# Every SBUF operand at a multiple of 128 bytes, and fourteen layouts for the operands of a squared-ReLU MLP

## The chip, the cores and the metric

The kernel runs on one core of one Trainium2 chip. The core has TensorE (PE in the profile), VectorE (DVE), ScalarE (ACT), GpSimd (POOL) and SyncE (SP, which issues most DMAs). On-chip memory is SBUF, 128 partitions wide; TensorE accumulates in PSUM. The metric is the device time of one execution in microseconds (us). Before the change it is 448.87 us, the median of three runs (448.64 to 449.05).

A matmul here has two operands in SBUF. The *stationary* one, 128 x 128 numbers, is loaded into the array by a weight load (LDWEIGHTS, the row PEld of the profile); the *moving* one, 128 partitions x N columns, is streamed through it by the MATMUL. Every matmul of this kernel is preceded by a weight load of its own.

## The reference: what is computed

Two blocks read the same x (2048 tokens, width 448), and a gate mixes them:

```python
g = sigmoid((x * gate_w).sum(-1, keepdims=True))
a = linear_attention(x, wqkv, wo)         # 16 heads, phi(t) = max(t,0) + min(exp(t),1) + 1e-6
h = relu(x @ w1 + b1) ** 2                # 448 -> 1792
b = h @ w2 + b2                           # 1792 -> 448
out = g * a + (1 - g) * b
```

All is float32. Each operand is split into a high part, rounded to the type float32r, and a low part that holds the rest; a product is then three matmuls (high x high, high x low, low x high).

## The kernel before

**Tiling.** Tokens go in four blocks b of 512. The 1792 hidden features are fourteen feature tiles f of 128, and each block meets them in two halves of seven (NH = 7): first b = 0, 1, 2, 3 with f = 0 to 6, then b = 3, 0, 1, 2 with f = 7 to 13.

**The two MLP products.** `up(b, f)` (line 206) makes `h_ps`: the stationary operand is a 128-column piece of `w1`, the moving one `xh` or `xl`, 512 columns; eleven matmuls. `hidden` takes ReLU (line 210) and square (211) on ACT and splits the result into `hh` and `hl` on DVE (a cast by line 59, a subtraction by line 62). `down(b, f)` (line 235) adds into `o_ps`: for each of four token tiles the stationary operand is 128 columns of `hh` or `hl`, the moving one a half of `w2_f`, 448 columns; twelve matmuls. So each feature tile has 4 x 11 = 44 matmuls up and 4 x 12 = 48 down, and the fourteen together 616 and 672.

**The other products** run by line 74: keys `k_ps` (176 matmuls of 450 columns), the Gram products `g_ps` (176 of 448), queries `q_ps` (160 of 512), the attention output `a_ps` (176 of 448), and some small ones: `m_ps` and `d_ps`, and by lines 356 and 335 `kv_ps` (32 of 112) and `z_ps`.

**Order.** The instruction order on every engine is fixed when the program is built. TensorE works on `up(b, f)`, then on `down(b, f - 1)`, then on a piece of the attention block; in the second half it is `denominators`, `scaled` and `attention`. DVE, ACT and SP follow in the same order, each engine strictly one instruction after the other. An instruction that waits for a semaphore holds up everything behind it on its engine.

**Memory.** Long-lived tiles lie in the pool `keep`, one after the other. Loaded raw data and short-lived results share the pool `work`: NSLOT = 16 slots of 2048 bytes a partition. Whoever takes a slot waits until the last reader of its previous content is done. `tmp` and later `late` hold the operands of the attention block.

**Where the operands start.** Byte addresses in a partition, modulo 128, as the built program has them:

| operand | stationary or moving | before | after |
|---|---|---|---|
| `xh`, `xl` | moving in up and q, stationary in k | 0 | 0 |
| `w1`, tiles fl = 0 to 3 of a half | stationary | 0 | 0, 16, 32, 48 |
| `w1`, tiles fl = 4 to 6 | stationary | 64 | 64, 80, 96 |
| `hh`, `hl` | stationary | 96 | 0 |
| `w2_f` | moving | 0 | by f, see the change |
| `wq_s` | stationary | 96 | 0 |
| `m_s` (a) | moving | 0, 8, 16, 24, 32, 40, 48 by piece | 0 |
| `qh`, `ql` (a) | stationary | 96 | 0 |
| `wk_s` (k) | moving | 0, 8, ... 48 by piece | the same |
| `nh`, `nl` (g) / `ph`, `pl` | stationary / moving | 96 / 96 | 0 / 0 |

Of the kernel before, what the change touches and what calls it, by code (L numbers as in the profile page):

```python
# [7 lines left out]
F = mybir.dt.float32  # L8
R = mybir.dt.float32r
# [4 lines left out]
S, D, FF, H = 2048, 448, 1792, 16  # L14
DH = D // H
P = 128
# [14 lines left out]
def gated_mix_kernel(ctx: ExitStack, tc: tile.TileContext, xt, xn, wk, wq, wv, wo, w1a, w1b, w2, b1, b2, hmask,  # L31
# [2 lines left out]
    act, dve, pool, pe, sp = nc.scalar, nc.vector, nc.gpsimd, nc.tensor, nc.sync  # L34

    keep = ctx.enter_context(tc.tile_pool(name="keep", bufs=1))
    work = ctx.enter_context(tc.tile_pool(name="work", bufs=1, side="right"))
    acc_p = ctx.enter_context(tc.tile_pool(name="acc_p", bufs=4, space=PSUM))
    mm_p = ctx.enter_context(tc.tile_pool(name="mm_p", bufs=2, space=PSUM))
    ms_p = ctx.enter_context(tc.tile_pool(name="ms_p", bufs=2, space=PSUM))  # L40

    NSLOT, NLATE = 16, 15

    def slot(shape, dt, name):
        return work.tile(shape, dt, name=name, tag="s", bufs=NSLOT)
# [77 lines left out]

    def split_w1(h, g, c, hi_eng=act):
        if c == 0:
            w1_s[h, g] = keep.tile([P, 7, (TB, 3 * P)[g]], R, name=f"w1_{h}{g}", tag=f"w1{g}", bufs=1)
        split_w(w1_s[h, g], c, w1_raw.pop((h, g, c)), hi_eng, dve)

    w2_s, w2_raw = {}, {}

    def load_w2(f):
# [1 line left out]
        load(w2_raw[f], w2[f])  # L133

    def split_w2(f):
        w2_s[f] = keep.tile([P, 2, D], R, name=f"w2_{f}", tag="w2", bufs=NH)
        split_hi(act, w2_s[f][:, 0], w2_raw[f])
        split_lo(dve, w2_s[f][:, 1], w2_raw.pop(f), w2_s[f][:, 0])

    xn_raw = {}  # L140

# [16 lines left out]
    for _ in range(18):  # L158
        pe.matmul(warm_ps[:, :256], warm[:, :P], warm, start=True, stop=True)

    side = keep.tile([P, 2], F, name="side")
    dve.memset(side[:64, 0:1], -1.0)
    dve.memset(side[:64, 1:2], 0.0)
    dve.memset(side[64:], 1.0)
# [1 line left out]
    for c in range(4):  # L166
# [3 lines left out]
            load_x(0, c, TB // 2, TB)  # L170
        else:
            load_x(0, c)
    b1_s = keep.tile([P, NF], F, name="b1_s")
    load(b1_s, b1)
    load_w2(0)
    load_w2(1)
# [2 lines left out]

    b2_s = keep.tile([P, D], F, name="b2_s")  # L180
    hm = keep.tile([P, P], R, name="hm")
    half = keep.tile([P, 2], F, name="half")
    ones = keep.tile([P, 2], F, name="ones")
    dve.memset(ones, 1.0)
    ksum = keep.tile([P, D], F, name="ksum")
    logit = keep.tile([P, NT], F, name="logit")
    gate = keep.tile([P, 2, NT], F, name="gate")
    part = [keep.tile([P, D], F, name=f"part{t}") for t in range(NT)]

# [6 lines left out]
    def up_chunk(ps, b, f, c):  # L196
        h, fl = divmod(f, NH)
        g, i = divmod(fl, 4)
        w, cols = w1_s[h, g], slice(i * P, (i + 1) * P)
        xh, xl = xs[b]  # L200
        if c < 3:
            terms = [(w[:, c, cols], xh[:, c]), (w[:, c, cols], xl[:, c]), (w[:, 4 + c, cols], xh[:, c])]
        else:
            terms = [(w[:, 3, cols], xh[:, 3]), (w[:, 3, cols], xl[:, 3])]
        for n, (a, m) in enumerate(terms):
            pe.matmul(ps, a, m, start=(c == 0 and n == 0), stop=(c == 3 and n == 1))  # L206

    def hidden(ps, b, f):
        r = slot([P, TB], F, f"hr{b}_{f}")
        act.activation(r, ps, AF.Relu, bias=b1_s[:, f:f + 1])  # L210
        act.activation(r, r, AF.Square)  # L211
        h = slot([P, TB], R, f"hh{b}_{f}")
        lo = slot([P, TB], R, f"hl{b}_{f}")
        split_hi(dve, h, r)
        split_lo(dve, lo, r, h)
        hs[f] = (h, lo)

    def up(b, f):
        ps = mm_p.tile([P, 512], F, name=f"h_ps{b}_{f}", tag="mm")
# [4 lines left out]
    o_ps = {}  # L224

    def down(b, f, tiles=range(4)):
        h, lo = hs[f]
        w = w2_s[f]
        for i in tiles:
            if f % NH == 0:  # L230
                o_ps[i] = acc_p.tile([P, 512], F, name=f"o_ps{b}_{f}_{i}", tag="acc")
            cols = slice(i * P, (i + 1) * P)
            terms = [(h[:, cols], w[:, 0]), (h[:, cols], w[:, 1]), (lo[:, cols], w[:, 0])]
            for n, (a, m) in enumerate(terms):
                pe.matmul(o_ps[i][:, :D], a, m, start=(f % NH == 0 and n == 0),  # L235
                          stop=(f % NH == NH - 1 and n == 2))
# [83 lines left out]
        split_lo(dve, second[0], second[1], second[0])  # L320


    zc = keep.tile([P, 4], F, name="zc")

# [173 lines left out]
    for f in range(2, 4):  # L500
        hidden(first[f], 0, f)

    wk_s = keep.tile([P, 7, D + 2], R, name="wk_s", tag="wkm", bufs=1)

    load_xn(0)
    load_w2(2)
# [108 lines left out]
    for n, b in enumerate(order):  # L615
        then = order[n + 1] if n + 1 < NB else None
        for f in range(NF - NH, NF):
            fl = f - NH
            run_todo()
            up(b, f)  # L620
            if fl:
                if n + 1 < NB or f + 1 < NF:
                    down(b, f - 1)
            elif n == 0:
                down(b, NH - 1)
                half_done(b)
            else:
                down(order[n - 1], NF - 1)
                for i in range(4):
                    finish(order[n - 1], i)  # L630
            if n == 0:
                if fl < 4:
                    todo += queries(b, (3, 0, 1, 2)[fl])
                if fl == 0:
                    for c in range(4):
                        load_w1(1, 1, c)
                    kv_product()
                    phase1.close()
                    late = ctx.enter_context(tc.tile_pool(name="late", bufs=1, side="right", reuse_waits="tile"))
                    m_s = keep.tile([P, 7, 450], R, name="m_s", tag="wkm", bufs=1)  # L640
                    for j in range(2):
                        load_wo(j)
                if fl == 1:
                    for c in range(4):
                        split_w1(1, 1, c)
                if fl in (1, 2):
                    for j in range(2 * fl - 2, 2 * fl):
                        split_wo(j)
                        todo += m_product(j)
                    if fl == 1:  # L650
                        for j in range(2, 4):
                            load_wo(j)
                if fl < 2:
                    load_w2(NH + 5 + fl)
                    split_w2(NH + 4 + fl)
                if fl == 2:
                    split_w2(NH + 6)
                if fl == 4:
                    todo += denominators(b)
                if fl == 5:  # L660
                    for c in range(4):
                        scaled(b, c)
                if fl == 6:
                    for i in range(4):
                        attention(b, i)
            else:
                if fl == 0:
                    todo += denominators(b)
                if fl == 1:
                    for c in range(4):  # L670
                        scaled(b, c)
                if 2 <= fl < 6:
                    attention(b, fl - 2)
            if then is not None:
                if fl < 2:
                    load_x(then, 2 * fl)
                    load_x(then, 2 * fl + 1)
                if 1 <= fl < 3:
                    split_x(then, 2 * fl - 2)
                    split_x(then, 2 * fl - 1)  # L680
                if n and 3 <= fl:
                    todo += queries(then, (3, 0, 1, 2)[fl - 3])
                if n == 0 and fl in (5, 6):
                    for c in ((3, 0), (1, 2))[fl - 5]:
                        todo += queries(then, c)
# [56 lines left out]
```

## Time and profile before

| | |
|---|---|
| median of three runs | 448.87 us |
| the profiled execution | 448.76 us |
| its span (first to last instruction) | 447.0 us |
| PE busy | 439.9 us, 2054 matmuls |
| PEld busy | 381.2 us |
| DVE / ACT / POOL busy | 267.8 / 172.4 / 58.5 us |
| granted TensorE clock | 0.999 |

The profiled execution lies 0.11 us under the median, inside the spread of the runs. Outside the span lie 1.8 us. In the profile a row names source line, engine, operation and tiles (`o_ps<-w,hh` reads `w2` and `hh` and writes `o_ps`; the numbers of blocks and tiles are left out), then shapes and a count. The recorded duration of a matmul (368 or 394 ns) is a latency, from its start to the end of its drain: matmuls overlap, and what one costs is the distance from its start to the next one's start. The chain of waits gives such distances directly: a piece of the chain with its start, its length and the count of instructions in it.

### The profile page before, as it was taken

To read this page: it belongs to the slowest core of one execution; us is meant where nothing else is said; L and a number is where in the kernel's file an instruction comes from. 1 tells how busy PE (TensorE), PEld (TensorE's weight loads), DVE (VectorE), ACT (ScalarE), POOL (GpSimd) and SP (SyncE) were. 2 spreads that over 40 slices of the span, in tenths; PEclk is the share of its full clock that TensorE was granted. 3 is DMA by queue.
4 is the path that set the end of the run, shared out by engine and by line. 5 is a ranking of instruction groups with operands and counts; after the bars stand their busy time and mean duration, and the time that the engine had idled before them with its cause. 6 is when DMAs were issued, how large, how long until landed. Compare 5 with 4: busy or idle time off the path is not lost.

```text
span 447.0 us, 5489 instructions
## 1 busy us (share of the span) xinstructions
PE 439.9 (98%) x2054; PEld 381.2 (85%) x2054; DVE 267.8 (60%) x452; ACT 172.4 (39%) x298; POOL 58.5 (13%) x75
## 2 busy tenths in 40 slices
PE   8999999999999999999999989999999999999996
PEld 6888898888888888888888868888888898888885
DVE  5968445442687326772466678788355974549423
ACT  5945235331455123542344334335232443234221
POOL 0243124110342005320002420000000000000000
PEclk9999999999999999999999999999999999999999
DMA  7651210022031211252145311040100501002002
GB/s 270 186 179 52 84 44 25 23 65 70 0 116 31 66 44 40 70 137 55 42 123 146 72 37 24 1 165 12 26 0 0 177 1 25 0 0 84 0 1 82
DMA packets 18315, 28.77 MB, mean 64 GB/s; under 512 B 2880, under 2 KB 12784, under 8 KB 18288
## 3 DMA queue, kind: packets, MB, share of 16 engines
q1 hardware_dynamic: 17072, 26.81, 19.7%
q0 software_dynamic: 1216, 1.61, 1.9%
q8 instruction: 16, 0.26, 0.3%
q14 instruction: 11, 0.09, 0.1%
HBM read 22.09 MB, written 3.67 MB: 58 GB/s over the span
## 4 chain that ended last, share of the span: by engine, by line
PE 93%; DVE 3%; ACT 2%; issue 1%; DMA 1%; SPq 0%; DVEq 0%; ACTq 0%
PE h_ps L206 30%; PE o_ps L235 30%; PE q_ps L74 8%; PE a_ps L74 8%; PE g_ps L74 8%; PE k_ps L74 7%; PE kv_ps L356 1%; DMA xr<-in_xt 1%; ACT hr L210 1%; PE m_ps L74 1%; DVE hh L59 0%; ACT hr L211 0%; DVE r L254 0%; ACT ph L55 0%; DVE r L255 0%
## 5 line engine op out<-in xcount | busy, mean ns | idle before, releaser
L235 PE MATMUL o_ps<-w,hh 128*128 128x448 f32 x448 | 127.9, 368 | 0.5 <-DVE hh L59 0.5
L206 PE MATMUL h_ps<-xh,w 128*128 128x512 f32 x392 | 127.9, 394 | 0.2
L235 PEld LDWEIGHTS o_ps<-w,hh 128*128 128x128 f32 x448 | 84.0, 188 | 11.8 <-DVE hh L59 1.2
L206 PE MATMUL h_ps<-xl,w 128*128 128x512 f32 x224 | 88.2, 394 | 0.0
L206 PEld LDWEIGHTS h_ps<-xh,w 128*128 128x128 f32 x392 | 73.7, 188 | 16.5 <-ACT xh L55 0.6
L235 PE MATMUL o_ps<-w,hl 128*128 128x448 f32 x224 | 80.8, 369 | 0.0
L210 ACT ACTIVATE hr<-h_ps,b_s 128x512 f32<-128x512 f32 x56 | 38.2, 683 | 101.7 <-PE h_ps L206 99.9
L59 DVE CAST hh<-hr 128x512 fp32r<-128x512 f32 x56 | 25.3, 451 | 43.1 <-ACT hr L211 42.4
L206 PEld LDWEIGHTS h_ps<-xl,w 128*128 128x128 f32 x224 | 42.1, 188 | 8.7
L235 PEld LDWEIGHTS o_ps<-w,hl 128*128 128x128 f32 x224 | 42.1, 188 | 4.2 <-DVE hl L62 0.2
L62 DVE TENSOR_TENSOR hl<-hr,hh 128x512 fp32r<-128x512 f32 x56 | 40.2, 718 | 2.0
L211 ACT ACTIVATE hr<-hr 128x512 f32<-128x512 f32 x56 | 35.2, 629 | 1.3
L74 PE MATMUL k_ps<-wk_s,xh 128*128 128x450 f32 x112 | 33.6, 366 | 0.0
L74 PE MATMUL q_ps<-xh,wq_s 128*128 128x512 f32 x100 | 33.5, 395 | 0.0
L74 PE MATMUL a_ps<-m_s,qh 128*128 128x448 f32 x112 | 32.6, 365 | 0.0
L62 POOL TENSOR_TENSOR nl<-xnr,nh 128x384 fp32r<-128x384 f32 x16 | 18.8, 1177 | 96.6 <-ACT nh L55 96.6
L473 DVE SCALAR_TENSOR_TENSOR part<-part,gate,u 128x448 f32<-128x448 f32 x16 | 10.9, 683 | 26.5 <-ACT u L472 26.5
L276 POOL TENSOR_TENSOR ksum<-ksum,r 128x448 f32<-128x448 f32 x15 | 18.9, 1262 | 53.2 <-DVE r L255 53.2
L472 ACT ACTIVATE u<-a_ps,gate 128x448 f32<-128x448 f32 x16 | 10.1, 634 | 38.3 <-PE a_ps L74 38.3
L254 DVE TENSOR_SCALAR r<-k_ps 128x448 f32<-128x448 f32 x16 | 10.0, 622 | 24.1 <-ACT e L253 24.1
L74 PE MATMUL g_ps<-pl,nh 128*128 128x448 f32 x64 | 23.4, 366 | 0.3 <-DVE pl L62 0.3
L74 PE MATMUL q_ps<-xl,wq_s 128*128 128x512 f32 x60 | 23.7, 395 | 0.0
(103 smaller groups left out, 562.4 us busy)
## 6 DMA issues: line engine op xcount, KB each, us to landing
xr<-in_xt SPq DMA_DIRECT2D x27, 256.0 KB, 3.0
xnr<-in_xn SPq DMA_DIRECT2D x16, 224.0 KB, 2.6
out<-out SPq DMA_DIRECT2D x16, 224.0 KB, 2.0
w2r<-in_w SPq DMA_DIRECT2D x14, 224.0 KB, 2.7
w1r<-in_w1a SPq DMA_DIRECT2D x8, 256.0 KB, 3.1
w1r<-in_w1b SPq DMA_DIRECT2D x8, 192.0 KB, 3.2
m_s<-m POOLq DMA_DIRECT2D x12, 112.0 KB, 2.7
wqr<-in_wq SPq DMA_DIRECT2D x4, 256.0 KB, 3.6
```

What stands on the lines that cost most here:

```text
L59: eng.tensor_copy(hi, src)
L62: eng.tensor_tensor(lo, src, f32(hi), op=ALU.subtract)
L74: pe.matmul(out_ps, a, b, start=(i == 0), stop=(i == n - 1))
L206: pe.matmul(ps, a, m, start=(c == 0 and n == 0), stop=(c == 3 and n == 1))
L210: act.activation(r, ps, AF.Relu, bias=b1_s[:, f:f + 1])
L211: act.activation(r, r, AF.Square)
L235: pe.matmul(o_ps[i][:, :D], a, m, start=(f % NH == 0 and n == 0), stop=(f % NH == NH - 1 and n == 2))
L254: dve.tensor_scalar(r, ps, 0.0, 1e-6, op0=ALU.max, op1=ALU.add)
L276: pool.tensor_tensor(ksum, ksum, p, op=ALU.add)
L356: pe.matmul(kv_ps[:JE, js], wv_s[c][:, js], gsum[c][:, js], start=(c == 0), stop=(c == 3))
L472: act.activation(u, ps[:, :D], AF.Copy, scale=gate[:, 0, t:t + 1])
L473: dve.scalar_tensor_tensor(part[t], part[t], gate[:, 1, t:t + 1], u, op0=ALU.mult, op1=ALU.add)
```

## The change

Four edits; no arithmetic is changed, and on every engine the same instructions stand in the same order as before.

1. **Sizes are rounded so that all tiles start at multiples of 128 bytes.** Small tiles get 128 bytes each, `side` moves into a pool of its own, `wk_s` and `m_s` get a common tile of 3168 elements, and the rows of `m_s` are 448 elements instead of 450. The room for it comes from `work`: NSLOT falls from 16 to 14.
2. **Up: the 128-column pieces of `w1` lie 132 columns apart** (528 bytes), the second group starting at column 16. So the piece of feature tile fl starts 16 x fl bytes after a multiple of 128.
3. **Down: `w2_f` lies differently for each f** (`W2_AT`): f = 0 to 7 start 16 x f bytes after a multiple of 128; f = 8 and 9 at 0; f = 10 and 11 ("lines", at 0 and 64 bytes) are stored so that a matmul reads 16 bytes, steps 128 bytes on, reads 16 bytes, and so on, fourteen times, and then starts again one 16-byte piece further; f = 12 ("halves") has the high and low half interleaved in pieces of 64 bytes; f = 13 starts at 8 bytes.
4. **Down: `hh` and `hl` of f = 8 and 9 are stored with the token tiles interleaved** (`H_STEP`): for f = 8 the 128 columns of a stationary operand lie 4 elements (16 bytes) apart, for f = 9 they lie 2 elements (8 bytes) apart. DVE writes `hh` and `hl` with that step and reads `hh` with it.

The diff (line numbers of the kernel after it lie some 8 to 32 higher):

```diff
--- before.py
+++ after.py
@@ -34,12 +34,20 @@
     act, dve, pool, pe, sp = nc.scalar, nc.vector, nc.gpsimd, nc.tensor, nc.sync
 
     keep = ctx.enter_context(tc.tile_pool(name="keep", bufs=1))
+    rest = ctx.enter_context(tc.tile_pool(name="rest", bufs=1, side="right"))
     work = ctx.enter_context(tc.tile_pool(name="work", bufs=1, side="right"))
     acc_p = ctx.enter_context(tc.tile_pool(name="acc_p", bufs=4, space=PSUM))
     mm_p = ctx.enter_context(tc.tile_pool(name="mm_p", bufs=2, space=PSUM))
     ms_p = ctx.enter_context(tc.tile_pool(name="ms_p", bufs=2, space=PSUM))
 
-    NSLOT, NLATE = 16, 15
+    NSLOT, NLATE = 14, 15
+    LINE = 128
+    def small(n, dt, name):
+        return keep.tile([P, LINE // 4], dt, name=name)[:, :n]
 
     def slot(shape, dt, name):
         return work.tile(shape, dt, name=name, tag="s", bufs=NSLOT)
@@ -123,9 +131,16 @@
 
     def split_w1(h, g, c, hi_eng=act):
         if c == 0:
-            w1_s[h, g] = keep.tile([P, 7, (TB, 3 * P)[g]], R, name=f"w1_{h}{g}", tag=f"w1{g}", bufs=1)
-        split_w(w1_s[h, g], c, w1_raw.pop((h, g, c)), hi_eng, dve)
-
+            w1_s[h, g] = keep.tile([P, 7, (544, 416)[g]], R, name=f"w1_{h}{g}", tag=f"w1{g}", bufs=1)
+        a, n = ((0, 4), (16, 3))[g]
+        w = w1_s[h, g][:, :, a:a + 132 * n].rearrange("p c (i k) -> p c i k", k=132)[:, :, :, :P]
+        split_w(w, c, w1_raw.pop((h, g, c)).rearrange("p (i k) -> p i k", k=P), hi_eng, dve)
+    W2_AT = [(4 * k, "") for k in range(8)] + [(0, ""), (0, ""), (0, "lines"), (16, "lines"), (0, "halves"), (2, "")]
+    H_STEP = {8: 4, 9: 2}
     w2_s, w2_raw = {}, {}
 
     def load_w2(f):
@@ -133,9 +148,21 @@
         load(w2_raw[f], w2[f])
 
     def split_w2(f):
-        w2_s[f] = keep.tile([P, 2, D], R, name=f"w2_{f}", tag="w2", bufs=NH)
-        split_hi(act, w2_s[f][:, 0], w2_raw[f])
-        split_lo(dve, w2_s[f][:, 1], w2_raw.pop(f), w2_s[f][:, 0])
+        w = keep.tile([P, 2 * D + 32], R, name=f"w2_{f}", tag="w2", bufs=NH)
+        a, order = W2_AT[f]
+        w = w[:, a:a + 2 * D]
+        raw = w2_raw.pop(f)
+        if order == "halves":
+            w = w.rearrange("p (n s k) -> p s n k", s=2, k=16)
+            raw = raw.rearrange("p (n k) -> p n k", k=16)
+        elif order == "lines":
+            w = w.rearrange("p (s l b e) -> p s b l e", s=2, b=8, e=4)
+            raw = raw.rearrange("p (b l e) -> p b l e", b=8, e=4)
+        else:
+            w = w.rearrange("p (s n) -> p s n", s=2)
+        w2_s[f] = w
+        split_hi(act, w[:, 0], raw)
+        split_lo(dve, w[:, 1], raw, w[:, 0])
 
     xn_raw = {}
 
@@ -158,7 +185,7 @@
     for _ in range(18):
         pe.matmul(warm_ps[:, :256], warm[:, :P], warm, start=True, stop=True)
 
-    side = keep.tile([P, 2], F, name="side")
+    side = rest.tile([P, 24], F, name="side")[:, :2]
     dve.memset(side[:64, 0:1], -1.0)
     dve.memset(side[:64, 1:2], 0.0)
     dve.memset(side[64:], 1.0)
@@ -170,7 +197,7 @@
             load_x(0, c, TB // 2, TB)
         else:
             load_x(0, c)
-    b1_s = keep.tile([P, NF], F, name="b1_s")
+    b1_s = small(NF, F, "b1_s")
     load(b1_s, b1)
     load_w2(0)
     load_w2(1)
@@ -179,11 +206,11 @@
 
     b2_s = keep.tile([P, D], F, name="b2_s")
     hm = keep.tile([P, P], R, name="hm")
-    half = keep.tile([P, 2], F, name="half")
-    ones = keep.tile([P, 2], F, name="ones")
+    half = small(2, F, "half")
+    ones = small(2, F, "ones")
     dve.memset(ones, 1.0)
     ksum = keep.tile([P, D], F, name="ksum")
-    logit = keep.tile([P, NT], F, name="logit")
+    logit = small(NT, F, "logit")
     gate = keep.tile([P, 2, NT], F, name="gate")
     part = [keep.tile([P, D], F, name=f"part{t}") for t in range(NT)]
 
@@ -196,7 +223,8 @@
     def up_chunk(ps, b, f, c):
         h, fl = divmod(f, NH)
         g, i = divmod(fl, 4)
-        w, cols = w1_s[h, g], slice(i * P, (i + 1) * P)
+        w, cols = w1_s[h, g], slice(16 * g + i * 132, 16 * g + i * 132 + P)
         xh, xl = xs[b]
         if c < 3:
             terms = [(w[:, c, cols], xh[:, c]), (w[:, c, cols], xl[:, c]), (w[:, 4 + c, cols], xh[:, c])]
@@ -211,9 +239,12 @@
         act.activation(r, r, AF.Square)
         h = slot([P, TB], R, f"hh{b}_{f}")
         lo = slot([P, TB], R, f"hl{b}_{f}")
-        split_hi(dve, h, r)
-        split_lo(dve, lo, r, h)
-        hs[f] = (h, lo)
+        k = H_STEP.get(f, 1)
+        hv, lv = [t.rearrange("p (j c i) -> p j i c", c=P, i=k) for t in (h, lo)]
+        src = r.rearrange("p (j i c) -> p j i c", c=P, i=k)
+        split_hi(dve, hv, src)
+        split_lo(dve, lv, src, hv)
+        hs[f] = [(hv[:, i // k, i % k], lv[:, i // k, i % k]) for i in range(4)]
 
     def up(b, f):
         ps = mm_p.tile([P, 512], F, name=f"h_ps{b}_{f}", tag="mm")
@@ -224,13 +255,12 @@
     o_ps = {}
 
     def down(b, f, tiles=range(4)):
-        h, lo = hs[f]
         w = w2_s[f]
         for i in tiles:
             if f % NH == 0:
                 o_ps[i] = acc_p.tile([P, 512], F, name=f"o_ps{b}_{f}_{i}", tag="acc")
-            cols = slice(i * P, (i + 1) * P)
-            terms = [(h[:, cols], w[:, 0]), (h[:, cols], w[:, 1]), (lo[:, cols], w[:, 0])]
+            h, lo = hs[f][i]
+            terms = [(h, w[:, 0]), (h, w[:, 1]), (lo, w[:, 0])]
             for n, (a, m) in enumerate(terms):
                 pe.matmul(o_ps[i][:, :D], a, m, start=(f % NH == 0 and n == 0),
                           stop=(f % NH == NH - 1 and n == 2))
@@ -320,7 +350,7 @@
         split_lo(dve, second[0], second[1], second[0])
 
 
-    zc = keep.tile([P, 4], F, name="zc")
+    zc = small(4, F, "zc")
 
 
 
@@ -500,7 +530,8 @@
     for f in range(2, 4):
         hidden(first[f], 0, f)
 
-    wk_s = keep.tile([P, 7, D + 2], R, name="wk_s", tag="wkm", bufs=1)
+    wkm = keep.tile([P, 3168], R, name="wk_s", tag="wkm", bufs=1)
+    wk_s = wkm[:, :7 * (D + 2)].rearrange("p (c n) -> p c n", c=7)
 
     load_xn(0)
     load_w2(2)
@@ -637,7 +668,8 @@
                     kv_product()
                     phase1.close()
                     late = ctx.enter_context(tc.tile_pool(name="late", bufs=1, side="right", reuse_waits="tile"))
-                    m_s = keep.tile([P, 7, 450], R, name="m_s", tag="wkm", bufs=1)
+                    m_s = keep.tile([P, 3168], R, name="m_s", tag="wkm", bufs=1)
+                    m_s = m_s[:, :7 * D].rearrange("p (c n) -> p c n", c=7)
                     for j in range(2):
                         load_wo(j)
                 if fl == 1:
```

## The prediction

> **What bounds the kernel now.** I read the page first (its busy times, the granted clock and the chain that ended last), and then that chain in order of time.
>
> ```profile
> span 447.0 us, 5489 instructions
> PE 439.9 (98%) x2054; PEld 381.2 (85%) x2054; DVE 267.8 (60%) x452; ACT 172.4 (39%) x298; POOL 58.5 (13%) x75
> PEclk9999999999999999999999999999999999999999
> PE 93%; DVE 3%; ACT 2%; issue 1%; DMA 1%; SPq 0%; DVEq 0%; ACTq 0%
> ```
>
> TensorE is the bound, at its full clock, and it hardly waits; the chain is TensorE for 93%. No matmul is added or taken away, so the time changes by what one matmul costs from start to start, and by new stalls. The costs stand in the chain: length over count. First a stretch of the middle:
>
> ```profile
> 144.91 2.44 PE g_ps L74 x12
> 147.35 2.56 PE h_ps L206 x11
> 149.91 2.48 PE o_ps L235 x12
> ...
> 168.93 2.24 PE k_ps L74 x11
> 171.17 2.54 PE h_ps L206 x11
> 173.71 2.48 PE o_ps L235 x12
> ```
>
> Then the whole chain's longest pieces:
>
> ```profile
> 224.52 3.14 PE kv_ps L356 x32
> ...
> 232.70 2.57 PE q_ps L74 x11
> ...
> 274.58 8.94 PE a_ps L74 x44
> ```
>
> So o costs 206.7 ns (2.48 / 12), h 232.7 where its weight piece starts at 64 (the piece at 147.35 is f = 4) and 230.9 where it starts at 0 (171.17, f = 1), q 233.6, g 203.3, k 203.6, a 203.2. From o to q, 64 columns more cost 26.9 ns, 0.42 a column: 448 columns are 188 ns by that, 512 are 215, and every matmul carries 10 to 20 ns on top. That surcharge is all that the change can win on TensorE. It is not fixed. Near the start, where up runs alone and both operands begin at 0, the timeline of TensorE shows:
>
> ```profile
> 7.94 0.39 PE L206 MATMUL h_ps<-xl,w 128*128 128x512 f32 x1
> ...
> 8.62 0.39 PE L206 MATMUL h_ps<-xl,w 128*128 128x512 f32 x1
> ...
> 9.30 0.39 PE L206 MATMUL h_ps<-xl,w 128*128 128x512 f32 x1
> ```
>
> Three matmuls take 0.68 us, 226.7 ns each, 6 ns less than the same matmul costs against a weight piece at 64. Early o matmuls, in the chain between 20 and 60 us, come down by as much, to 200:
>
> ```profile
> 26.00 2.00 PE o_ps L235 x10
> ```
>
> So the distance between the two operands modulo 128 matters: 0 gives 227 to 231 (512 columns), 32 and 64 give 233. But with the same addresses o costs 200 there and 206.7 later, so there is also a dependence on what went before.
>
> **The change, part by part.** The order of instructions is the same on all five engines.
>
> *Queries.* Their distance goes from 32 to 0. 160 matmuls at 233.6 go to between 226.7 and 230.9; the middle, 229, gives 160 x 4.6 = -0.7 us.
>
> *Down, 672 matmuls at 206.7.* Nine of the fourteen tiles only get a new distance (0, 16, ... 112, and 8). The lower bound is 200 (26.00), the upper no change. The nearest rows are a and k, whose moving pieces lie at seven offsets in steps of 8: 203.2 and 203.6. I take 204 for all fourteen tiles, before any price of a column order: 672 x 2.7 = -1.8 us (bounds -4.5 and 0).
>
> *Up, 616 matmuls.* Tiles that were at 0 move to 0, 16, 32 and 48, tiles at 64 to 64, 80 and 96. Some lose the good distance, some the bad one. Bounds 226.7 and 233.6 against a mean of 231.7, thus -3.1 to +1.2 us; I take 0, as four tiles of seven leave 230.9 or stay there, and three leave 232.7 or stay there.
>
> *a, g, k, m, d, kv.* a goes from mixed offsets to 0, where g is already; 203.2 against 203.3: 0. In the others both operands move together: 0.
>
> *f = 8, stationary columns 16 bytes apart.* No row shows a strided operand of TensorE. What a load costs now is shown by kv, bound by its loads of 112 columns: 3.14 us / 32 = 98 ns, thus 112 ns for 128 columns (an estimate by proportion). It hides under a matmul of 204. Lower bound: the same 112, cost 0. Upper bound: each column takes as long as the four that it now skips over, 448 ns, which the matmul can't hide: 48 x (448 - 204) = 11.7 us. I take the middle ratio, a doubled load of 224 ns: 48 x 20 = +1.0 us. f = 9, 8 bytes apart: 112 to 224 by the same reasoning, thus 0 to +1.0; halfway it stays under 204, so 0. [...]
>
> *f = 10, 11 and 12, moving operand in pieces.* [...] Upper bound: the stream halves, 144 x 188 = +27 us. I take 0, for lack of any row in which whole 16-byte pieces cost; a price per jump is a rival.
>
> *DVE for f = 8 and 9.*
>
> ```profile
> L59 DVE CAST hh<-hr 128x512 fp32r<-128x512 f32 x56 | 25.3, 451 | 43.1 <-ACT hr L211 42.4
> ...
> L62 DVE TENSOR_TENSOR hl<-hr,hh 128x512 fp32r<-128x512 f32 x56 | 40.2, 718 | 2.0
> ```
>
> The cast beats the subtraction on the same 512 columns by 267 ns. Strided, I expect it to lose that, +0.27 us, and `hl` nothing; the bounds are 0, and twice the subtraction's price for both, which adds 1.0 and 0.7. TensorE feels it where DVE has no lead. That is in the last block, in the timeline of DVE:
>
> ```profile
> 408.41 0.36 DVE L59 CAST hh<-hr 128x512 fp32r<-128x512 f32 x1
> ...
> 409.28 0.68 DVE L62 TENSOR_TENSOR hl<-hr,hh 128x512 fp32r<-128x512 f32 x1
> ...
> 412.89 0.42 DVE L59 CAST hh<-hr 128x512 fp32r<-128x512 f32 x1
> 413.23 0.68 DVE L62 TENSOR_TENSOR ql<-qe,qh 128x512 fp32r<-128x512 f32 x1
> ```
>
> and of TensorE:
>
> ```profile
> 409.46 1.40 PE L235 MATMUL o_ps<-w,hh 128*128 128x448 f32 x6
> 410.70 0.78 PE L235 MATMUL o_ps<-w,hl 128*128 128x448 f32 x3
> ...
> 414.75 0.37 PE L74 MATMUL a_ps<-m_s,ql 128*128 128x448 f32 x1
> ```
>
> `hh` of f = 8 is done at 408.77, its first matmul starts at 409.46: a lead of 0.69, or 0.5 after the weight load before it. `hl` is done at 409.96 for 410.70; `ql` at 413.91 for 414.75. Behind `hh` on DVE stand `qe`, `hl` and the `ql` that attention waits for, so delays add up: 2 x 0.27 = 0.54 at `ql`, within the 0.6 there. So 0. At the upper bound DVE is 1.7 late after f = 8: a stall of some 1.1 us.
>
> *DVE and ACT for `w1` and `w2`.* Runs of 128 columns, or 16 bytes for two of fourteen `w2`; the latter are made a stage before their use: 0.
>
> *Two slots fewer.* I laid the new slots over the old times: who would find the last reader still at work? Loads mostly, and SP issues in order, so those behind them move too; nearly all keep a lead over their first reader. The tightest place is at 15 to 24 us. The load of the second `xn` tile, on SP:
>
> ```profile
> 15.64 0.33 SPq L48 DMA_DIRECT2D xnr<-in_xn  x1
> ```
>
> ```profile
> xnr<-in_xn SPq DMA_DIRECT2D x16, 224.0 KB, 2.6
> ```
>
> ```profile
> 18.31 0.58 PE L235 MATMUL o_ps<-w,hh 128*128 128x448 f32 x2
> ```
>
> It now takes the slot of `hh0_0`, which TensorE reads until 18.89, and lands at 21.5 instead of 18.2; ACT wants it at 20.88, so it is 0.6 us late. Behind it on ACT, and then on TensorE and DVE:
>
> ```profile
> 20.88 0.56 ACT L55 ACTIVATE nh<-xnr 128x448 fp32r<-128x448 f32 x1
> 21.58 0.55 ACT L253 ACTIVATE e<-k_ps 128x448 f32<-128x448 f32 x1
> ```
>
> ```profile
> 22.98 0.56 PE L235 MATMUL o_ps<-w,hh 128*128 128x448 f32 x2
> ...
> 31.17 0.39 PE L206 MATMUL h_ps<-xh,w 128*128 128x512 f32 x1
> ```
>
> ```profile
> 26.59 0.56 DVE L62 TENSOR_TENSOR w<-w1r,w 64x384 fp32r<-64x384 f32 x1
> ```
>
> The exponential of the first keys (21.58) now takes the slot of `hh0_1`, which TensorE reads until 23.54: ACT is held for 2.0 us, which covers the 0.6, and behind it stand the four splits of the second `w1` group, the last of which DVE ends at 27.15. Even 2 us later is 29.2, ahead of the matmul of 31.17 that needs it. So 0; without that cover, 2.0 us.
>
> **Sum.** -0.7 - 1.8 + 1.0 = -1.5 us: 448.76 becomes 447.3 for the profiled execution, 447.4 on the median of the runs, which lies 0.11 higher.
>
> **Rivals.**
> 1. *Strided loads are dear* (slower). Place: the 48 loads of f = 8. At the fourfold 448 ns the total is 447.4 + 10.7 = 458.1. It decides the sign once 48 x (load - 204) exceeds 2.5 us, a load above 256 ns, 2.3 times today's. For it: one of four elements is used. Against it: 92 ns of today's 204 are free.
> 2. *Jumps in the moving operand cost* (slower). At one column's time, 0.42 ns, for each of 111 jumps of "lines" (96 matmuls) and 27 of "halves" (48): 4.5 + 0.5 = +5.0, thus 452.4. It decides from 0.13 ns a jump. For it: every stream in the trace is unbroken, so none shows that jumps are free.
> 3. *Distance isn't the cause*, and the change of addresses does nothing: +1.0 alone, 449.9. For it: o at 200 and at 206.7 with the same addresses. Against it: 227 and 233 for h. [...]
> 4. *DVE writes at half rate*: the stall of 1.1 us in the last block on top, 448.5, no change. For it: the leads there are 0.5 to 0.8. Against it: everywhere else they are 2 us and more.
> 5. *All matmuls reach the good distance's price*, 226.7 and 200: 616 x 5.0 + 160 x 6.9 + 672 x 6.7 = 8.7 saved, 1.0 paid: 441.2. Against it: the offsets differ from tile to tile, so up and down can't have one distance throughout.
>
> **How the numbers follow.** Forecast 0.41, with its own range 445.3 to 448.4: below, down at 202.5 and f = 8 free (-0.7 - 2.8 = -3.5); above, down at 205.5 and f = 8 doubled (-0.7 - 0.8 + 1.0 = -0.5); rival 1 0.15, rival 2 0.13, rival 3 0.14, rival 4 0.13, rival 5 0.04. A measurement of this kernel tells about 0.2%, 0.9 us, from no change. Faster than that: 0.36 of the forecast, 0.01 of rival 4, and rival 5: 0.41. Within: 0.05 of the forecast, 0.04 of rival 3, 0.10 of rival 4: 0.19. Slower: 0.15 + 0.13 + 0.10 + 0.02 = 0.40. The range runs from 445.3, which leaves out rival 5 and a little of the forecast, to 458.5, which takes in rival 1's fourfold load and leaves out dearer streams: some 0.16 is left out.
>
> **What would show it.** In the chain after: q at 229 per matmul (11 in 2.52), a and g at 203; the o pieces of f = 0 to 7 and 13 between 200 and 206.7, differing by f; f = 8 at 224 or so (12 in 2.69), which at 448 ns would be 5.4 us and name rival 1; f = 10 and 11 like the others, or 45 ns dearer for rival 2; casts of `hh` for f = 8 and 9 at 0.69. If waits of TensorE for `hh`, `hl` or `ql` appear at 408 to 416, it is rival 4; if the chain at 20 to 30 us holds ACT's exponential, a slot was missed. I am wrong if o's cost doesn't depend on f, or if a column order costs more than all offsets win.

## The result: 451.77 us, 0.56% slower

| | before | after |
|---|---|---|
| median | 448.96 us (448.64 to 449.46, 4 runs) | 451.77 us (451.46 to 451.89, 4 runs) |
| ratio | | 1.0056, 95% interval 1.0038 to 1.0074 |
| the profiled execution, its span | 448.76, 447.0 us | 451.46, 449.7 us |

The forecast was 447.4; the time lies inside the range and on the other side of the old one. The page after (its busy times, the clock and the engines' shares of the chain) is the old picture, 2.7 us longer:

```profile
span 449.7 us, 5472 instructions
PE 442.4 (98%) x2054; PEld 384.7 (86%) x2054; DVE 271.3 (60%) x452; ACT 172.5 (38%) x298; POOL 57.5 (13%) x75
PEclk9999999999999999999999999999999999999999
PE 93%; DVE 3%; ACT 2%; DMA 1%; issue 1%; SPq 0%; DVEq 0%; ACTq 0%
```

TensorE is still the bound at its full clock (granted 1.000, and 0.999 before), so the time went into what one matmul costs. The chain after, in order of time (start us, length us, what): first one block's seven down tiles, f = 0 to 6, with the up piece ahead of f = 0 (that of up's f = 1) and ahead of f = 4 (up's f = 5):

```profile
65.70 2.56 PE h_ps L234 x11
68.26 2.44 PE o_ps L265 x12
...
75.52 2.47 PE o_ps L265 x12
...
82.78 2.48 PE o_ps L265 x12
...
90.06 2.45 PE o_ps L265 x12
...
94.94 2.55 PE h_ps L234 x11
97.49 2.40 PE o_ps L265 x12
...
104.92 2.45 PE o_ps L265 x12
...
113.98 2.46 PE o_ps L265 x12
```

then queries and attention, and down's f = 8 (304.95), 10 (319.07), 11 (329.00), 12 (338.89), 13 (346.53) and 7 (352.02):

```profile
233.10 2.56 PE q_ps L82 x11
...
275.39 9.08 PE a_ps L82 x44
...
304.95 2.78 PE o_ps L265 x12
...
319.07 2.55 PE o_ps L265 x12
...
329.00 2.56 PE o_ps L265 x12
...
338.89 2.52 PE o_ps L265 x12
...
346.53 2.47 PE o_ps L265 x12
...
352.02 2.43 PE o_ps L265 x12
```

Where unbroken pieces of twelve o matmuls took 2.45 to 2.48 before, they now run from 2.40 (f = 4, 64 bytes) over 2.55 (the two "lines" tiles) to 2.78 (f = 8). Up now costs 231.0 to 233.5 ns a matmul, by tile, wherever its piece of `w1` starts; before it cost 229.6 at the good offset (0) and 233.2 at the bad one (64).

The whole difference, from the distance between the starts of successive matmuls, summed by product (after less before):

| part | us | ns a matmul, before and after |
|---|---|---|
| down, nine unbroken tiles (f = 0 to 7, 13) | -0.74 | 204.8-206.5, 200.4-206.4 |
| down f = 8 (16-byte steps) | +1.22 | 206.1, 231.6 |
| down f = 9 (8-byte steps) | -0.05 | 204.9, 203.8 |
| down f = 10, 11 ("lines"), 12 ("halves") | +0.36, +0.32, +0.18 | 204.9, 206.4, 206.2; 212.5, 213.0, 210.0 |
| up, after its first 44 matmuls | +0.34 | 231.1, 232.1 (all of up) |
| up, the first 44, with the waits for data among them | +0.41 | |
| start of the first up matmul, 5.22 to 5.52 us | +0.30 | |
| queries | -0.09 | 233.2, 232.6 |
| attention, Gram, keys | +0.27, +0.13, +0.09 | 203.2, 202.9, 204.0; 204.8, 203.6, 204.4 |
| sum | +2.74 | |

The two rows on the start of up, 0.71 us together, can't be put down to the change: as the experiments show, both differ by as much between kernels in which up is laid out alike.

Below, "ns a matmul" is always the mean start-to-start distance of the matmuls named, stalls (250 ns and more) left out. "Distance" is the moving operand's address in bytes less the stationary one's.

### The profile page after: what moved, and what is told of

Read it like the earlier page. It is cut to its first block, busy times and chain, and to the rows that moved or that the text cites. A ratio compares the mean times of both kernels' runs of the same rounds, so it can differ in the third digit from the quotient of the medians.

```text
span 449.7 us, 5472 instructions
## 1 busy us (share of the span) xinstructions
PE 442.4 (98%) x2054; PEld 384.7 (86%) x2054; DVE 271.3 (60%) x452; ACT 172.5 (38%) x298; POOL 57.5 (13%) x75
## 4 chain that ended last, share of the span: by engine, by line
PE 93%; DVE 3%; ACT 2%; DMA 1%; issue 1%; SPq 0%; DVEq 0%; ACTq 0%
PE h_ps L234 30%; PE o_ps L265 30%; PE q_ps L82 8%; PE a_ps L82 8%; PE g_ps L82 8%; PE k_ps L82 7%; DMA xr<-in_xt 1%; PE kv_ps L386 1%; ACT hr L238 1%; PE m_ps L82 1%; ACT hr L239 0%; DVE r L285 0%; DVE r L284 0%; PE d_ps L82 0%; DVE hh L67 0%
## 5 line engine op out<-in xcount | busy, mean ns | idle before, releaser
L265 PEld LDWEIGHTS o_ps<-w,hh 128*128 128x128 f32 x448 | 86.8, 199 | 10.7 <-DVE hh L67 1.1
L67 DVE CAST hh<-hr 128x512 fp32r<-128x512 f32 x56 | 26.3, 469 | 44.2 <-ACT hr L239 43.8
L265 PEld LDWEIGHTS o_ps<-w,hl 128*128 128x128 f32 x224 | 44.0, 199 | 3.7 <-DVE hl L70 0.2
L70 DVE TENSOR_TENSOR hl<-hr,hh 128x512 fp32r<-128x512 f32 x56 | 43.6, 779 | 1.9
L70 POOL TENSOR_TENSOR nl<-xnr,nh 128x384 fp32r<-128x384 f32 x16 | 17.2, 1072 | 96.6 <-ACT nh L63 96.6
```

What stands on the lines that cost most here:

```text
L67: eng.tensor_copy(hi, src)
L70: eng.tensor_tensor(lo, src, f32(hi), op=ALU.subtract)
```

## Experiments

Two theories stood at the beginning. **A**: each tile's price depends on how its two operands lie to each other, so the parts add up and can be undone one by one. **C**: the addresses of unbroken operands don't matter on average, and only the column orders cost. Later expectations add **B** (the neighbouring products set up's price), **D** (the alignment of the stationary operand alone counts) and others that they explain. All times below are medians, with the ratio to the kernel before measured beside them.

### All operands at 0, and then down at 64 bytes

```diff
-    W2_AT = [(4 * k, "") for k in range(8)] + [(0, ""), (0, ""), (0, "lines"), (16, "lines"), (0, "halves"), (2, "")]
-    H_STEP = {8: 4, 9: 2}
+    W2_AT = [(0, "")] * 14      # e4_down64: [(16, "")] * 14
+    H_STEP = {}
-            w1_s[h, g] = keep.tile([P, 7, (544, 416)[g]], ...)
+            w1_s[h, g] = keep.tile([P, 7, (TB, 3 * P)[g]], ...)     # dense 128-column pieces at 0
```

> The change without its layouts: every operand starts at a multiple of 128 bytes, w1 pieces lie 128 columns apart in rows of 512 and 384 columns as before the change, all fourteen w2 tiles start at 0, no interleaving. Theory A (the cost of a matmul is set by the distance of its operands modulo 128, as read off the changed kernel): o at 203.5 ns as f = 0 there, h at 229.6 as the pieces at 0 had before, against 206 and 231.7 before: 672 x 2.5 + 616 x 2.1 = 3.0 us under the kernel before, about 446. Theory C (on average the addresses of unbroken operands don't matter, some 18 ns on top of the columns whatever they are; only the column orders cost): o at 206, h at 232, within 0.5 us of the kernel before, about 449.

> As the plain kernel (all operands at multiples of 128 bytes, no column orders), but all fourteen w2 tiles start at 64 bytes, the offset of the cheapest tile of the changed kernel (f = 4, 200.4 ns). Theory A: o at 200.4 ns for all 672, 2.1 us under the plain kernel and about 4 to 5 us under the kernel before, 444 to 445. Theory C: f = 4 was a chance of its history; o at 204 to 206 ns and no difference from the plain kernel.

446.33 us (445.71 to 447.12), ratio 0.9945 [0.993, 0.996]; and 445.07 us (444.54 to 445.61), 0.9916 [0.9901, 0.9931]. As A said, and C is out. The same two pieces (up's f = 1, down's f = 0) in the kernel with all at 0:

```profile
65.24 2.52 PE h_ps L234 x11
67.77 2.43 PE o_ps L265 x12
```

and with `w2` at 64 bytes:

```profile
64.76 2.49 PE h_ps L234 x11
67.25 2.41 PE o_ps L265 x12
```

With all at 0, up costs 228.6 ns on the mean of its fourteen tiles and down 203.4; with `w2` at 64 bytes down falls to 201.3. So edit 1 alone makes the kernel faster, and edits 2 to 4 more than use that up.

### The changed kernel without the steps, and without the pieces

```diff
-    H_STEP = {8: 4, 9: 2}
+    H_STEP = {}                        # e2_no_step
```

```diff
-    W2_AT = [...] + [(0, ""), (0, ""), (0, "lines"), (16, "lines"), (0, "halves"), (2, "")]
+    W2_AT = [...] + [(0, ""), (0, ""), (0, ""), (0, ""), (0, ""), (2, "")]      # e3_no_pieces
```

> The changed kernel with hh and hl of f = 8 and 9 stored in order again. If the 16-byte step of the stationary operand costs what the trace shows for f = 8 (231.6 against 206 ns, 48 times), this is 1.2 us under the changed kernel, about 450.5, and f = 8 at 203 to 206 ns with a weight load recorded at 188 ns instead of 330. If f = 8 is dear for another reason (its place in the order), it stays at 231 ns and the time at 451.8.

> The changed kernel with w2 of f = 10, 11 and 12 in order at 0, nothing else undone. If the moving operand in pieces is what makes these three dear (212.5, 213.0, 210.0 against 205.8 ns), they fall to about 204 and the time by 1.1 us, to about 450.7. If it is their place in the order, they stay at 210 to 213 ns and the time at 451.8.

449.55 us (449.24 to 451.91), ratio 1.0025 [1.0011, 1.0038]; 449.79 us (449.34 to 451.39), 1.0027 [1.0017, 1.0037]. The chain: without the steps, f = 8; without the pieces, f = 10:

```profile
358.03 2.44 PE o_ps L265 x12
```

```profile
318.19 2.44 PE o_ps L265 x12
```

Both gain about 2 us on the median of ten runs, where 1.1 to 1.3 was expected; a few of the ten lie near the changed kernel's time. By the starts, f = 8 fell from 231.6 to 203.5 ns, 48 x 28.1 = 1.35 us, and the three ordered tiles by 8.9, 10.3 and 6.2 ns, together 1.22 us. The rest is not in the edited tiles: in the first 44 up matmuls 11.55 became 11.09 us without the steps, and the first up matmul started at 5.33 and 5.16 instead of 5.52. That start lay between 4.73 and 5.78 over all kernels tried, without order, and the first 44 up matmuls took between 10.80 and 11.87 us: 11.55, 11.09 and 11.53 in the changed kernel and these two, which differ only in tiles of down that come later. Both are scatter.

### Up: the pieces or the rows?

```diff
-            w1_s[h, g] = keep.tile([P, 7, (544, 416)[g]], ...)      # e5_w1_dense: on the changed kernel
+            w1_s[h, g] = keep.tile([P, 7, (TB, 3 * P)[g]], ...)
```

```diff
-            w1_s[h, g] = keep.tile([P, 7, (TB, 3 * P)[g]], ...)     # on the kernel with all at 0
+            w1_s[h, g] = keep.tile([P, 7, (544, 416)[g]], ...)      # e6_w1_pitch
+            w1_s[h, g] = keep.tile([P, 7, (576, 448)[g]], ...)      # e10_rows_576
```

> The changed kernel, but the weight pieces of up stand side by side again, 128 columns each from offset 0 in rows of 512 and 384; the down tiles keep their offsets, column orders and steps. In the changed kernel h costs 231 to 233 ns at every offset, also at offset 0, and in the kernel with all operands at 0 and dense pieces it costs 228.6. Theory A (the rows and gaps of w1 cost up 3.4 ns a matmul, and the tiles do not influence each other): 616 x 3.4 = 2.1 us off, 451.8 becomes 449.7, with h at 228 to 230 for all f and o per tile as in the changed kernel (f = 4 200.4, f = 10 212.5). Theory B (h is slow because its neighbours, the down tiles, have mixed offsets): h stays near 232 and the time stays at 451.5.

> The kernel with all operands at 0, in order and without steps, in which only the rows of w1 get the changed kernel's lengths of 544 and 416 columns; the pieces themselves stay dense from offset 0. It splits the 3.4 ns of up between the row length and the 16-byte offsets of the pieces. Theory A1 (the offsets of the pieces cost it): as the kernel with all at 0, 446.3, h 228.6. Theory A2 (the row length costs it: in the changed kernel even f = 0, whose offset is 0, costs 232): 446.3 + 2.1 = 448.4, h near 232.

> As the kernel with w1 rows of 544 and 416 columns, but with rows of 576 and 448, whole multiples of 256 bytes as 512 and 384 are; the pieces stay dense at offset 0. By the allocation f = 0 to 3 of each half get distance 0 modulo 256 and f = 4 to 6 get 128 throughout. Theory P256: f = 0 to 3 and 7 to 10 cost 228.6, f = 4 to 6 and 11 to 13 cost 232.4 as the queries do. Theory R (any row length other than 512 or 384 costs, for another reason): all fourteen near 232. Theory P128 (the row length does not count modulo 128 and something else was slow): all at 228.6.

449.98 us (449.42 to 451.47), ratio 1.0026 [1.0012, 1.0041]: with dense pieces in the changed kernel up is back at 228.8, so B is out. The down tiles did not all keep their prices, as A had expected: the shorter `w1` moved their distances by 128 bytes, and f = 4, now at 192, costs 201.9 instead of 200.4, f = 13, now at 136, 212.1 instead of 205.9. 448.01 us (447.61 to 449.97), 0.9983 [0.9968, 0.9998]: with every piece at 0 modulo 128, rows of 544 and 416 columns alone make up cost 231.8. A2 holds in that the row length is enough; what the 16-byte offsets would cost in rows of 512 wasn't run, and the 233.1 ns that an offset of 32 bytes costs under "Up's curve" speaks against their being free. Then 446.71 us (446.49 to 447.57), 0.9953 [0.9938, 0.9968], with rows of 576 and 448. The chain of the kernel with rows of 544, the up pieces of f = 13 and 7:

```profile
334.31 2.56 PE h_ps L234 x11
...
341.85 2.55 PE h_ps L234 x11
```

and of the one with 576 and 448, the same two:

```profile
334.39 2.55 PE h_ps L234 x11
...
341.93 2.49 PE h_ps L234 x11
```

Rows of 576 columns (9 x 256 bytes) are good, rows of 544 (8.5 x 256 bytes) are not, and the group that the allocation put 128 bytes off stays dear: 229.0 ns for f = 0 to 3 and 7 to 10, 232.3 for f = 4 to 6 and 11 to 13. P256: the distance counts modulo 256, and with rows of 544 it alternates from one chunk to the next. Alternating itself costs something too: the mean of the two prices would be 230.3 (six matmuls at 228.6, five at 232.3), and 231.8 was measured. In that kernel the matmuls on either side of a change from 0 to 128 cost 233.8 and 234.2 ns, those within a run at 0 cost 228.8, and those within a run at 128 cost 232.6.

### Down: which operand must be where?

```diff
+    rest = ctx.enter_context(tc.tile_pool(name="rest", bufs=1, side="right"))     # e8_slots_64: on the kernel before
     work = ctx.enter_context(tc.tile_pool(name="work", bufs=1, side="right"))
...
+    rest.tile([P, 8], F, name="gap")
```

> The kernel before with one thing added: 32 bytes between the slots and what lies above them, so that all slots begin at 64 modulo 128 instead of 96. Nothing else moves; w2 stays at 0, so down's distance between the two operands goes from 32 to 64. Theory A (the distance modulo 128 sets down's price; 64 gave 201.0 to 201.9 in the kernel with w2 at 64 and slots at 0): 672 x (206 - 201.3) = 3.2 us off, 448.9 becomes 445.7; a moves by its own distances, some 0.3 either way. Theory D (what counts is that a stationary operand begins at a multiple of 128, as in all kernels tried with slots at 0): no change, 448.9, o near 206.

445.58 us (445.43 to 445.75), ratio 0.992 [0.9898, 0.9942]. One shift of 32 bytes, and 3.6 us are gone (the kernel before took 449.14 in the same session). The attention block's operands, which lie in the pools below the slots, move along, and attention's price went from 203.2 to 203.6 ns, so the gain isn't there. The chain, down's f = 0, then up's f = 5 and down's f = 4:

```profile
67.53 2.40 PE o_ps L237 x12
...
93.96 2.56 PE h_ps L208 x11
96.52 2.40 PE o_ps L237 x12
```

Down went from 205.8 to 200.5 ns, while up's f = 5, still at its old place, stays at 2.56 (232.9 ns on the mean of its group, f = 4 to 6 and 11 to 13). Once `w2` moved (all at 64) and once the slots, and down came to 201.3 and 200.5 ns: the relation of the two operands counts, D is out, and so is the prediction's rival 3.

### More strided tiles

```diff
-    H_STEP = {}                          # on the kernel with all at 0
+    H_STEP = {2: 4, 5: 4, 8: 4, 9: 2, 12: 2}
```

> The kernel with all operands at 0, with stationary columns 16 bytes apart in three tiles (f = 2, 5 and 8) and 8 bytes apart in two (f = 9 and 12). If the load is what costs, each of the three pays as f = 8 did, 48 x 28 ns = 1.35 us against its own 203.5, and the two pay nothing: 446.3 + 4.05 = 450.4, o of f = 2, 5 and 8 at 231.5, of f = 9 and 12 at 203.5. If f = 8 was special by its place in the order, f = 2 and 5 cost less than half of that: under 449.5.

451.30 us (451.0 to 451.7), ratio 1.0042 [1.0023, 1.0061]. In its chain f = 2, 5 and 8:

```profile
83.21 2.77 PE o_ps L265 x12
...
105.57 2.81 PE o_ps L265 x12
...
360.01 2.81 PE o_ps L265 x12
```

231.2, 234.3 and 234.1 ns, against 205.0 and 204.0 for the two 8-byte tiles. The price goes with the 16-byte step. The time was to be 450.4: by the starts the three tiles added 4.8 us instead of 4.05, part of it in a longer stall at f = 5 (matmuls of 250 ns and more take 1.6 us there, 1.1 with all at 0). The likely reason for the price is seen in the changed kernel's weight loads at f = 8, behind a last load of up:

```profile
358.72 0.19 PEld L234 LDWEIGHTS h_ps<-xh,w 128*128 128x128 f32 x1
358.95 1.49 PEld L265 LDWEIGHTS o_ps<-w,hh 128*128 128x128 f32 x6
...
361.51 0.33 PEld L265 LDWEIGHTS o_ps<-w,hl 128*128 128x128 f32 x1
```

One load is recorded with 0.33 us instead of 0.19, and six in a row take 1.49: (1.49 - 0.33) / 5 = 232 ns from load to load, which is the tile's price. That the matmuls wait for the loads is a reading: loads and matmuls come in turn, so the distance alone can't tell which waits, but of the two the load is the one whose operand changed and whose record grew, from 0.19 to 0.33.

### Up's curve

```diff
+            a = {(0, 0): 8, (0, 1): 16, (1, 0): 24, (1, 1): 0}[h, g]     # on the kernel with all at 0
-            w1_s[h, g] = keep.tile([P, 7, (TB, 3 * P)[g]], ...)
+            w1_s[h, g] = keep.tile([P, 7 * (TB, 3 * P)[g] + 32], ...)[:, a:a + 7 * (TB, 3 * P)[g]].rearrange("p (c n) -> p c n", c=7)
```

> The kernel with all operands at 0, whose w1 tiles, with dense pieces and rows of 512 and 384, begin at other places: the distance modulo 256 is 224 for f = 0 to 3, 64 for 4 to 6, 160 for 7 to 10 and 128 for 11 to 13. It gives the curve of up that goes with down's. Known are 0 (228.6) and 192 (233.2). Theory P256: 128 near 232.4, 64 near 233, 160 and 224 between 229 and 234. Theory P128: 128 is the same as 0, 228.6, and 64 the same as 192, 233.2. Theory R: all at 228.6.

447.77 us (447.29 to 448.42), ratio 0.9975 [0.9963, 0.9987]. Its chain, up at 224 (f = 2), at 64 (f = 5) and at 128 (f = 13):

```profile
72.18 2.57 PE h_ps L235 x11
...
94.08 2.52 PE h_ps L235 x11
...
333.64 2.56 PE h_ps L235 x11
```

128 is dear and 64 is not 192, so P128 and R are out. P256 had 64 near 233, and it cost 229.8: the period is right, the shape within it was not foreseen. With the other kernels this gives, in ns a matmul by the distance modulo 256 (where a row has several distances, in their order):

| distance | up, queries (512 columns) | down (448 columns) |
|---|---|---|
| 0 | 228.6 to 229.6; queries 227.8 | 203.0, 203.3 |
| 8, 16 | | 205.9, 202.5 |
| 32, 48 | queries 233.2 | 205.8 to 206.4, 203.1 |
| 64 | 229.8 | 200.2, 200.4, 200.5, 200.8 |
| 80, 96, 112 | | 202.8, 205.2, 205.8 |
| 128 | 232.3, 232.9; queries 232.3 to 232.9 | 203.5 to 203.9 |
| 136, 144 | | 212.1, 205.5 |
| 160, 176 | 233.2 at 160 | 203.4, 204.1 |
| 192 | 232.9, 233.2 | 202.0 |
| 208, 224, 240 | 233.1 at 224 | 203.8, 204.9, 202.7 |

In the column for down, the rows from 8 to 48 (but for 32), 80 to 112, 136 to 176 and 208 to 240 rest on one tile for each distance, and differences of 2 or 3 ns among them may come from neighbours: the Gram products, at distance 0 in all fourteen kernels, cost between 202.7 and 205.4. The steps between 0, 32 and 64, each measured on many tiles, are beyond that doubt.

### Pieces of the moving operand

```diff
-    W2_AT = [(0, "")] * 14               # on the kernel with all at 0; "piece/spacing" in bytes
+    W2_AT = [(0, o) for o in ("", "16/128", "", "", "16/64", "", "", "16/32", "", "", "64/128", "", "128/256", "")]
```

> The kernel with all operands at 0 and without steps, in which five w2 tiles are streamed in pieces: 16 bytes every 128 (f = 1, the changed kernel's lines), 16 every 64 (f = 4), 16 every 32 (f = 7), 64 every 128 (f = 10, the changed kernel's halves) and 128 every 256 (f = 12). It asks what of a column order costs. Theory J (each jump costs): 16-byte pieces the same at all three spacings, some 212.5, 64-byte pieces a quarter of the surcharge, 128-byte pieces an eighth. Theory W (a wider spacing costs, the jumps do not): f = 1 and 10 alike at 210 to 213, f = 4 at some 208, f = 7 at 205, f = 12 the dearest. Theory M (what the order breaks is the distance between stream and load, so each order only gets some price between today's best and worst unbroken ones and a little above): all five between 205 and 214 without order by jumps or spacing. Time by any of them 446.3 + 0.8 to 2.0 = 447.1 to 448.3.

446.35 us (446.25 to 446.99), ratio 0.9945 [0.993, 0.9959], where 447.1 to 448.3 was expected. By the starts its o rose by 0.62 us, less than the 0.8 to 2.0 expected, and other parts hide it: in the profiled executions (446.74 with all at 0, 446.99 here) the first 44 up matmuls took 0.45 longer and the later ones 0.50 less, as the kernel with all at 0 waited twice for `hh` (0.9 us) and this one once (0.5). The chain: f = 0 (unbroken), 1 and 4, then 10, 12 and 7:

```profile
68.18 2.43 PE o_ps L264 x12
...
75.39 2.52 PE o_ps L264 x12
...
97.27 2.46 PE o_ps L264 x12
...
316.70 2.48 PE o_ps L264 x12
...
336.25 2.48 PE o_ps L264 x12
...
349.23 2.44 PE o_ps L264 x12
```

16-byte pieces cost 209.9 ns at 128 bytes' spacing, 205.5 at 64 and 203.4 at 32, where unbroken tiles cost 202.7 to 203.9; 64-byte pieces at 128 cost 206.7, 128-byte pieces at 256 cost 206.6. Theory J is out: 111 jumps of 32 bytes cost next to nothing (203.4 ns, against 202.6 for the same tile unbroken). W is half right: a wider spacing costs more for the same piece, but f = 12 is not the dearest, and f = 1 and 10 are not alike. M, which had all five at 205 and more, fails on f = 7.

### All distances chosen

Distances fixed modulo 256: down and attention 64, up and queries 0.

```diff
-    w = keep.tile([P, 2 * D + 32], ...)                     # e9_best: on the kernel with all at 0
+    w = keep.tile([P, 2 * D], ...)
-    side = rest.tile([P, 24], F, name="side")[:, :2]
+    side = rest.tile([P, 40], F, name="side")[:, :2]
-    wq_s = keep.tile([P, 7, TB], R, name="wq_s")
+    wq_s = keep.tile([P, 7 * TB + 64], R, name="wq_s")[:, 32:32 + 7 * TB].rearrange("p (c n) -> p c n", n=TB)
+    n, a = (TB, 3 * P)[g], (0, 32)[g]
-    w1_s[h, g] = keep.tile([P, 7, (TB, 3 * P)[g]], ...)
+    w1_s[h, g] = keep.tile([P, 7 * n + 2 * a], ...)[:, a:a + 7 * n].rearrange("p (c n) -> p c n", n=n)
```

> The kernel with all operands at 0, in order, without steps, with four address edits: slots 64 bytes further, w2 without its spare columns, wq 128 bytes further, and the tile of the second w1 group shifted to match. So all distances (moving address less stationary address) are fixed modulo 256: down 64, attention 64, queries 0 instead of 128, up 0. Theory P256 (the period of the distance is 256 bytes: up cost 228.6 at 0, but about 232 where rows of 544 columns make 0 and 128 alternate, and queries, with the same shapes, cost 232.4 at 128): q comes down to 228.6, 160 x 3.8 = 0.6 us, and o to 200.5, 672 x 2.8 = 1.9 us, so 446.3 becomes 443.8. Theory P128 (the period is 128 bytes): q stays at 232.4, and the time is 444.4.

**442.50 us** (442.04 to 442.63), ratio 0.9853 [0.9836, 0.9869]: faster than both kernels, and by more than either theory gave. Its page and chain (down's f = 3, up's f = 5, attention, queries):

```profile
span 440.8 us, 5472 instructions
```

```profile
89.06 2.40 PE o_ps L266 x12
...
93.89 2.51 PE h_ps L235 x11
...
271.57 8.80 PE a_ps L82 x44
280.37 5.01 PE q_ps L82 x22
```

Queries went from 232.4 to 227.8 ns (22 took 5.01 us here), which P128 excludes; down costs 200.2, up 228.7, and attention, at distance 64 like down, fell from 203.6 to 200.2 unasked. The work after the first 44 up matmuls is 4.13 us shorter than with all at 0: down 2.04, queries 0.83, attention 0.60, up 0.45, the rest in keys, Gram and small products. Up's share is no price (228.6 and 228.7 ns): the kernel with all at 0 waited for `hh` once more.

## Why the prediction was wrong

Its frame held: TensorE bound at full clock (granted 1.000), no new stall after the start, everything in the surcharge of 10 to 20 ns. It was wrong in the rule for that surcharge, and in the two edits for which it took no price. The sum was -1.5 us and came out +2.7 in the span; the 4.2 us between come from these terms.

- **"The distance between the two operands modulo 128 matters: 0 gives 227 to 231."** That distance matters is right (32 bytes of shift: 3.6 us). The period is 256 for up and queries, and 0 is not down's best. The queries' term failed on it: their distance became 128 modulo 256, 232.6 ns instead of 229, -0.09 us instead of -0.7.
- **Down, -1.8.** Nine unbroken tiles gave 0.74; at 2.7 ns each they were to give 1.17. The mean of 204 was near (204.2), but by luck: the tiles span 200.4 to 206.4 as the curve says, and only f = 4 reached 64. What failed in the size is the old price: 206.7 was read from a few pieces of the chain, and over all of down it was 205.8, so the same 204 saves a third less.
- **"Up ... I take 0."** +0.34 after the start; the 0.41 in the first 44 matmuls is scatter. The term was costed by where a piece starts; the new row length of `w1`, in the same edit, was not costed at all, and it alone is enough to take the good price from every tile (228.6 against 231.8 ns with the pieces at 0). The piece at 147.35, read there as f = 4, is f = 5; both start at 64, so nothing hangs on it.
- **"f = 10, 11 and 12 ... I take 0."** +0.86, and 1.25 with the gain of 2.7 ns that these tiles were credited with: the largest miss. Rival 2 named the effect with 45 ns for "lines"; it is 7 to 10, and not a price per jump.
- **f = 8, "a doubled load of 224 ns".** Right in its condition (the 16-byte step) and nearly in size: 232 ns from load to load, 231.6 a matmul, +1.22 against the old tile where +0.87 was booked (1.0 less 48 x 2.7 ns). Rival 1's dear load is out: it needed 256. f = 9 at 0: 203.8 ns, right.
- **DVE.** The cast was to lose 0.27 us, and `hl` nothing. In the timeline of DVE in the last block, f = 8:

```profile
410.64 0.56 DVE L67 CAST hh<-hr 128x512 fp32r<-128x512 f32 x1
...
411.64 1.12 DVE L70 TENSOR_TENSOR hl<-hr,hh 128x512 fp32r<-128x512 f32 x1
```

  The cast lost 0.20 and the subtraction 0.44, so the second half was wrong. The cost of 0 stands: TensorE ran on, as its own timeline shows:

```profile
411.71 1.54 PE L265 MATMUL o_ps<-w,hh 128*128 128x448 f32 x6
413.09 0.86 PE L265 MATMUL o_ps<-w,hl 128*128 128x448 f32 x3
```

  `hh` is done at 411.20 for 411.71, `hl` at 412.76 for 413.09, and the six matmuls between start every 230 ns (1.38 us / 6): no stall, rival 4 is out.
- **Slots, 0.** No exponential of ACT stands in the chain between 20 and 30 us: right.
- **Attention, Gram, keys, 0.** +0.49. Attention cost 204.8 here and 204.2 and 203.5 in the two kernels that differ only in tiles of down; the same addresses, so at least 1.3 ns a matmul, 0.2 us, is scatter that no address edit explains. The rest of the 0.49 stays open.
- **Start, not in the sum.** +0.30, inside the scatter of 4.73 to 5.78.
- **Rival 5** (all at the good price, 441.2) was turned down because offsets differ from tile to tile. In this change they do; chosen freely they need not, and 442.50 is what that gives.

**Open.** Why 512 columns cost least at a distance of 0 (227.8 to 229.6 ns) and 448 columns at 64 (200.2 to 200.8) isn't shown. Nor is why the early o matmuls of the kernel before cost 200 ns at a distance of 32. The place within a piece counts as well: with all at 0 the first matmul of an up piece costs 231.1 ns and the last 226.7, at one distance. And the eight matmuls of `d_ps`, of 512 columns like up's, don't follow the table: 232.0 ns at a distance of 0 in the kernel before, 229.0 at 128 with all at 0.

## What to carry to other kernels

Where TensorE is the bound and every matmul has its own weight load, tabulate for each product the moving address less the stationary one modulo 256, over all chunks: a row length that isn't a multiple of 256 bytes spreads it. Shift one operand's tile by tens of bytes and read the start-to-start distances per tile; here one shift of 32 bytes was worth 0.8%, and all distances chosen, on top of edit 1, made 1.5%. Keep stationary columns close together (8 bytes apart they cost 203.8 to 205.0 ns here, like unbroken ones, and 16 bytes apart 231.2 to 234.3), and the moving operand unbroken or in pieces close together (16-byte pieces cost 203.4 ns at 32 bytes' spacing and 209.9 at 128).

## What the runs showed of the hardware that was not expected

- In up and the queries, of 512 columns, the price of a matmul depends on the operands' distance modulo 256: 227.8 to 229.8 ns at 0 and 64, 232.3 to 233.2 at 32, 128, 160, 192 and 224. For down's 448 columns the best is 64 (200.2 to 200.8 ns), the worst seen 136 (212.1, one tile).
- With stationary columns 16 bytes apart the loads follow each other every 232 ns, and a matmul costs 231 to 234 ns; 8 bytes apart it costs 203.8 to 205.0, like unbroken ones.
- DVE's cast and subtraction of 128x512 that write with a step of 16 bytes take 0.56 and 1.12 us in the last block, against 0.36 and 0.68 unbroken.
